# First batch reordered behind narrow dummies, second batch's turns up to one slot later, fourth and fifth batch's transfers held in turn

## The chip, the cores and the metric

The kernel runs on one core of a Trainium2 chip. The metric is the device time of one execution in microseconds (us). A profile times one execution from its first to its last instruction (the span, some 1.7 us less than the device time) and lists the TensorE clock that was granted. Ratios below are the mean time of one kernel's fast runs over the mean of the other's fast runs of the same rounds, so they are not quite the ratio of the medians quoted beside them. "Fast" is a state of the machine; every run quoted here counted as fast.

Short names: PE is TensorE, PEld its weight loads, DVE VectorE, ACT ScalarE, POOL GpSimd, SP SyncE. Batches are counted from one in the text and from zero in the code: the fifth batch is `b == 4`.

## The reference, cut

```python
q_p, k_p = phi(q, cos_w, sin_w), phi(k, cos_w, sin_w)    # relu, times cos and sin of the position
kv  = np.einsum('bhsf,bhsd->bhfd', k_p, v)                # 8 batches, 8 heads, 576 x 64
z   = np.sum(k_p, axis=2)
x   = num / den           # num: q_p with kv; den: q_p with z, + 1e-6
# x as 4608 tokens x 512, then 8 experts of 512 -> 1024 -> 512 on all tokens,
# weighted by a gate matrix that is normalised 8 times by row and by column
```

## The kernel before, the parts that matter

Attention of a batch is made while PE works on the first expert for the batch ahead of it. A block of that expert has 16 slots; `at(block, slot, fn, ...)` puts attention work behind a slot. From the third batch on, q_p is transposed by DMA; the first two batches use PE ("turns"). All six loads of a batch are issued by POOL, all transposes by SP.

The steps of a batch, in the words used below. VectorE makes q_p and k_p tiles from the loaded q and k (phi in the reference). Transposes put q_p's columns in front, and where PE does it, ScalarE or VectorE copies each turned tile out of PE's output memory (an eviction). The sums are PE's matmuls of k_p with copies of v. The denominators are its matmuls of the turned q_p with the sums of k_p; VectorE takes their reciprocal (`hl`), PE spreads it over all rows (the spread matmuls) and ScalarE copies that out (`rb`). The numerators are PE's matmuls of the turned q_p with the sums; VectorE multiplies them by rb into `xT`, which is what the expert's first layer reads (FFN; its second layer follows in the same block). `acc_lo` and `acc_hi` in the lines are storage lent to such tiles, v copies and turned q_p among them.

```python
qp_pool = p1.enter_context(tc.tile_pool(name="qp_pool", bufs=3))
...
def load(b, half, names="qkv", held_back=False):
    ...
    if held_back:
        after(ve.last, i)                     # the load waits for VectorE's instruction issued last
...
q_p = qp_pool.tile([P, C, 2, D], F16, name="q_p")         # one of three buffers
ve.tensor_tensor(out=q_p[:], ...)
if by_dma:                                                # b >= 2
    turned = nc.sync.dma_start(out=qTs[b, hk], in_=q_p..., transpose=True)
    if b == 3 and hk == 0:
        after(landing["v", b, 1], turned)                 # this transpose waits for the last v load
...
# second batch, beside the first block
for hk in range(HK):
    for i in range(3):
        at(0, (5, 6, 6, 7)[hk], turn, 1, hk, i, i != 1)
...
for half in range(2):
    at(0, 7, sums_first, half)
...
# fifth batch (j == 2): q_p, k, k_p and v by slot; numerators of the fourth batch
    (4, prep_q, 0), (5, prep_k, 0), (5, prep_q, 1), (6, prep_k, 1),
    (8, prep_q, 2), (8, prep_k, 2), (10, prep_q, 3), (10, prep_k, 3),
    (11, prep_kv, 0), (14, prep_kv, 1),
at(j, 9, numerators_of, b, 0, 1)
at(j, 13, numerators_of, b, 2, 3)
...
for name in "qkv":                                        # j == 1: the fifth batch's loads
    for half in range(2):
        at(j, 12, load, b + 2, half, name, True)
```

A transpose reads a q_p buffer, so the fourth q_p of a batch waits until the first transpose has landed and given its buffer back (VectorE waited 0.70 us for that ahead of 64.82 and 0.35 ahead of 82.86 in the profile of before).

The softmax here doesn't subtract the row's maximum and nothing guards it: scores larger than these inputs give would overflow.

## Time and profile before

| | before |
|---|---|
| median of the runs beside the change | 978.56 us (977.54 to 978.70) |
| span of the profiled run | 977.2 us, clock 1.00 |
| PE busy | 98% of the span |
| PE's first real turn | 8.62 us |
| first second-layer matmul | 34.46 us |
| fourth batch's last denominators | 73.81 us |
| fifth batch's first spread matmul | 97.02 us |

The last four rows are marks. From the last mark to the end of the span these two kernels and the others below take 880 us within 0.5, so a kernel's time is settled by its first 97 us. How to read the time-ordered list: start, length, engine, source line, operation, output and inputs, count, and in brackets how long the engine stood idle before and what ended it. These are VectorE's lines, and then PE's matmul that needs their result, around the fifth batch's last q_p in the kernel before:

```profile
82.86 0.76 DVE L109 TENSOR_TENSOR q_p<-q_ld,acc_hi 128x1152 f16<-128x1152 f16 x1 [0.35 <-DMA q_pT<-q_p]
...
85.45 1.55 DVE L109 TENSOR_TENSOR xT<-small_ps,rb 128x384 f16<-128x384 f32 x4 [0.80 <-PE small_ps L109]
...
87.34 2.80 PE L109 MATMUL h_ps<-xT,w1e 128*128 128x512 f16 x12
```

The q_p waits 0.35 us for a buffer, and VectorE is again idle for 0.80 us before it makes the last xT tiles. PE's matmul on those tiles starts at 87.34, without waiting.

### The profile page before, as it was taken

The numbers are of one execution on the slowest core, as the hardware profiler recorded it, in microseconds if no ns is written. First come the engines' busy times: TensorE is split into PE (matmuls) and PEld (weight loads), VectorE is DVE, ScalarE is ACT, GpSimd is POOL, SyncE is SP. The second block draws the span as 40 slices with busy tenths as digits, with TensorE's granted clock in tenths as the row PEclk, the third lists the DMA queues.
The fourth block names the chain that finished last, engine by engine and source line by source line (L and its number), as shares of the span: only waits on it lengthen the run. The fifth ranks groups of instructions, "written<-read, shape, count | busy, mean of one in ns | idle before, by whom it ended". The sixth has DMA issues, their size and how long they took to land.

```text
span 977.2 us, 20236 instructions
## 1 busy us (share of the span) xinstructions
PE 962.4 (98%) x7855; PEld 675.7 (69%) x7855; DVE 807.8 (83%) x1833; ACT 564.7 (58%) x1262; POOL 60.6 (6%) x82
## 2 busy tenths in 40 slices
PE   9999999999999999999999999999999999999997
PEld 6545555457777777777777777777777777777775
DVE  6767775888988887988888887988888888988887
ACT  5766665477776555555555555555555555555551
POOL 6231110010000000000000000000000000000001
PEclk9999999999999999999999999999999999999999
DMA  9999986330104401323104401323103401104435
GB/s 163 183 149 178 152 141 111 68 68 34 42 25 83 78 25 41 64 51 70 35 25 83 78 25 36 68 55 66 37 25 80 81 25 38 37 26 120 127 89 128
DMA packets 80336, 73.54 MB, mean 75 GB/s; under 512 B 33264, under 2 KB 72176, under 8 KB 80240
## 3 DMA queue, kind: packets, MB, share of 16 engines
q0 software_dynamic: 27232, 30.94, 20.3%
q1 hardware_dynamic: 52768, 41.06, 17.2%
q8 instruction: 61, 1.00, 0.4%
q14 instruction: 35, 0.29, 0.1%
q10 hardware_dynamic: 240, 0.26, 0.1%
HBM read 83.12 MB, written 12.98 MB: 98 GB/s over the span
## 4 chain that ended last, share of the span: by engine, by line
PE 88%; DMA 4%; DVE 3%; issue 2%; ACT 1%; POOL 1%; POOLq 0%; ACTq 0%; SPq 0%
PE rows_ps L109 33%; PE h_ps L109 26%; PE p_ps L109 11%; PE copied_ps L109 11%; PE y_ps L109 4%; PE small_ps L109 2%; DMA k_ld<-in_k_dram 1%; DMA w1e<-in_moe_w_dram 1%; DMA w2e<-in_moe_w_dram 1%; DMA acc_hi<-q_p 1%; DVE P_tok L109 1%; DVE colp L109 0%; POOL q_ld L202 0%; DVE rs L109 0%; DVE acc_hi L955 0%
## 5 line engine op out<-in xcount | busy, mean ns | idle before, releaser
L955 DVE SCALAR_TENSOR_TENSOR acc_lo<-rows_ps,P_tok,acc_lo 128x512 f32<-128x512 f32 (+1 forms) x322 | 203.9, 643 | 74.9 <-PE rows_ps L109 74.8
L109 PEld LDWEIGHTS <-H 128*128 128x128 f16 x2080 | 203.2, 98 | 82.5 <-issue 1.2
L891 ACT CAST u<-h_ps 128x384 f16<-128x384 f32 x288 | 138.0, 479 | 131.0 <-PE h_ps L109 131.0
L109 PEld LDWEIGHTS <-w1e 128*128 128x128 f16 x1632 | 157.7, 98 | 67.6 <-issue 5.3
L885 DVE CUSTOM_DVE_ANT_0 H<-p_ps,u 128x384 f16<-128x384 f32 x329 | 181.9, 553 | 6.5 <-PE p_ps L109 6.5
L109 PEld LDWEIGHTS <-hs 128*128 128x128 f16 x1500 | 146.6, 98 | 56.2
L109 PE MATMUL h_ps<-S,w1e 128*128 128x384 f16 x672 | 164.1, 326 | 0.7 <-ACT u L109 0.6
L109 PE MATMUL p_ps<-xT,T 128*128 128x384 f16 x672 | 164.1, 326 | 0.1
L109 PE MATMUL rows_ps<-V,H 128*128 128x256 f16 x1000 | 150.0, 273 | 0.7 <-DVE acc_hi L955 0.7
L109 PE MATMUL rows_ps<-w2e,hs 128*128 128x256 f16 x1000 | 150.0, 273 | 0.0
L109 PE MATMUL h_ps<-xT,w1e 128*128 128x384 f16 (+1 forms) x616 | 148.7, 350 | 0.1
L923 ACT ACTIVATE H<-h_ps 128x384 f16<-128x384 f32 x144 | 70.8, 492 | 95.0 <-PE h_ps L109 95.0
L109 PEld LDWEIGHTS <-T 128*128 128x128 f16 x1008 | 98.4, 98 | 30.2 <-issue 3.6
L109 PE MATMUL rows_ps<-w2e,H 128*128 128x256 f16 (+1 forms) x568 | 92.3, 285 | 0.0
L904 ACT COPY copied_ps<-h_ps 128x384 f32<-128x384 f32 x144 | 67.5, 469 | 35.4 <-PE h_ps L109 35.4
L914 ACT ACTIVATE H<-copied_ps 128x384 f16<-128x384 f32 x144 | 71.0, 493 | 20.3 <-PE copied_ps L109 20.3
L109 PE MATMUL h_ps<-S,T 128*128 128x384 f16 x336 | 81.8, 325 | 0.4 <-ACT copied_ps L109 0.3
L109 PE MATMUL copied_ps<-xT,w1e 128*128 128x384 f16 x336 | 82.1, 326 | 0.0
L109 PE MATMUL copied_ps<-w2e,H 128*128 128x256 f16 x504 | 75.5, 272 | 0.0
L109 PE MATMUL rows_ps<-V,hs 128*128 128x256 f16 x500 | 75.0, 272 | 0.0
L955 DVE SCALAR_TENSOR_TENSOR acc_lo<-copied_ps,P_tok,acc_lo 128x256 f32<-128x256 f32 x126 | 60.4, 480 | 0.6 <-PE copied_ps L109 0.2
L955 DVE SCALAR_TENSOR_TENSOR acc_hi<-rows_ps,P_tok,acc_hi 128x512 f32<-128x512 f32 (+1 forms) x56 | 41.4, 739 | 20.5 <-PE rows_ps L109 19.7
(145 smaller groups left out, 951.7 us busy)
## 6 DMA issues: line engine op xcount, KB each, us to landing
S<-x_saved SPq DMA_DIRECT2D x108, 192.0 KB, 2.4
out_dram<-acc_lo SPq DMA_DIRECT2D x62, 128.0 KB, 2.4
w1e<-in_moe_w_dram POOLq DMA_DIRECT2D x7, 1024.0 KB, 8.8
w2e<-in_moe_w_dram POOLq DMA_DIRECT2D x7, 1024.0 KB, 9.7
q_ld<-in_q_dram POOLq DMA_DIRECT2D x16, 288.0 KB, 7.1
k_ld<-in_k_dram POOLq DMA_DIRECT2D x16, 288.0 KB, 8.5
v_ld<-in_v_dram POOLq DMA_DIRECT2D x16, 288.0 KB, 9.6
x_saved<-S SPq DMA_DIRECT2D x18, 192.0 KB, 1.9
```

The source lines that it names most:

```text
L109: i = getattr(self.engine, name)(*args, **kwargs)
L885: latest = ve._custom_dve(TENSOR_ADD_SAT, out=out, in0=ps[:, 0:TU], in1=t[:], s0=FP32_MAX, s1=0.0)
L891: se.copy(out=t[:], in_=ps[:, 0:TU])
L904: se.copy(out=Y[:, 0:TU], in_=X[:, 0:TU])
L914: se.activation(out=h11, in_=Y[:, 0:TU], func=AF.Relu)
L923: se.activation(out=h12, in_=X[:, 0:TU], func=AF.Relu)
L955: ve.scalar_tensor_tensor(out=a, in0=rows, scalar=P_tok[:, g, self.e : self.e + 1], in1=a, op0=ALU.mult, op1=ALU.add,)
```

## The change

It has four parts: (a) 110 dummy matmuls of 64 columns for 74 of 128; (b) the first batch in a new order, with few dummies inside it; (c) the second batch's turns in slots 6, 6, 7, 7 for 5, 6, 6, 7, with the v copies in slot 7; (d) all four of the fourth batch's transposes wait for its last v load, the fifth batch's six loads wait for the last of these transposes, and some of its slots move. Its intent: start real work sooner, and keep transposes and loads from running through each other.

```diff
-        for _ in range(74):
-            keep_busy(1)
+        for _ in range(110):
+            te.matmul(out=idle_ps[:, 0:HP], lhsT=ones_sq[:],
+                rhs=ones_sq[:, 0:1].to_broadcast([P, HP]), start=True, stop=True)
 ...  # (b), cut: loads of q and k issued in another order, second half of k made positive
 ...  # after the first k_p tile and not the second, sums of the second
 ...  # half after the first spreads, k_p of the second batch behind the first batch's last xT
-                        at(0, (5, 6, 6, 7)[hk], turn, 1, hk, i, i != 1)
+                        at(0, (6, 6, 7, 7)[hk], turn, 1, hk, i, i != 1)
 ...
-                if held_back:
+                if behind is not None:
+                    after(turnings[behind], i)
+                elif held_back:
                     after(ve.last, i)
 ...
-                if b == 3 and hk == 0:
+                if b == 3:
                     after(landing["v", b, 1], turned)
+                turnings[b, hk] = turned
 ...
-                    (4, prep_q, 0), (5, prep_k, 0), (5, prep_q, 1), (6, prep_k, 1),
-                    (8, prep_q, 2), (8, prep_k, 2), (10, prep_q, 3), (10, prep_k, 3),
+                    (4, prep_q, 0), (5, prep_q, 1), (7, prep_k, 0), (8, prep_k, 1),
+                    (8, prep_q, 2), (9, prep_k, 2), (10, prep_q, 3), (10, prep_k, 3),
 ...
-                        at(j, 12, load, b + 2, half, name, True)
+                        at(j, 12, load, b + 2, half, name, True, (b + 1, HK - 1))
```

More of the change, by code (lines that the diff above doesn't have):

```diff
@@ L195, with load @@
         landing = {}
+        turnings = {}
         sources = {"q": q, "k": k, "v": v}
-        def load(b, half, names="qkv", held_back=False):
+        def load(b, half, names="qkv", held_back=False, behind=None):
             for name in names:
@@ L217 @@
         load(0, 0, "q")
+        load(0, 1, "q")
         gidx = cs_pool.tile([P, C], FP32, name="gidx")
@@ L222 @@
         )
+        load(0, 0, "k")
         ones_sq = cs_pool.tile([P, P], F16, name="ones_sq")
@@ L230 @@
         )
-        load(0, 1, "q")
-        for name in "kv":
-            load(0, 0, name)
-            load(0, 1, name)
+        load(0, 1, "k")
+        for half in range(2):
+            load(0, half, "v")
         w0 = new_weights(wA)
@@ L256 @@
         idle_ps = ps_y.tile([P, Dm], FP32, name="y_ps")
-        for _ in range(74):
-            keep_busy(1)
+        for _ in range(110):
+            te.matmul(
+                out=idle_ps[:, 0:HP], lhsT=ones_sq[:],
+                rhs=ones_sq[:, 0:1].to_broadcast([P, HP]), start=True, stop=True,
+            )
         wrap = cs_pool.tile([P, C], FP32, name="wrap")
@@ L275, with halve @@
         ve.memset(cs_half[:], 0.0)
-        for hh in range(2):
-            ve.tensor_copy(
-                out=cs_half[hh * HP : (hh + 1) * HP, :, :, hh],
-                in_=cs[hh * HP : (hh + 1) * HP, :, :, 0],
-            )
+        def halve():
+            for hh in range(2):
+                ve.tensor_copy(
+                    out=cs_half[hh * HP : (hh + 1) * HP, :, :, hh],
+                    in_=cs[hh * HP : (hh + 1) * HP, :, :, 0],
+                )
         early = cs_pool.tile([P, 1], FP32, name="early")
@@ L289 @@
         C3 = C // 3
+        ones_col = const.tile([P, 1], FP32, name="ones_col")
+        ve.memset(ones_col[:], 1.0)
+        ones_all = const.tile([P, P], FP32, name="ones_all")
+        ve.memset(ones_all[:], 1.0)
+        eps_row = cs_pool.tile([1, 32], FP32, name="eps_row")
+        ve.memset(eps_row[:], 1e-6 / XS)
+        lent = acc_lo[:, G_LO - 4 : G_LO, :].rearrange("p g d -> p (g d)").bitcast(F16)
+        VA = C * (D + 2)
+        v_augs = [
+            lent[:, i * VA : (i + 1) * VA].rearrange("p (c d) -> p c d", d=D + 2)
+            for i in range(4)
+        ]
+        for t in v_augs:
+            ve.memset(t[:, :, D : D + 1], 1.0 / XS)
         lo = cs_pool.tile([P, 1], FP32, name="lo")
@@ L308 @@
         )
-        ones_col = const.tile([P, 1], FP32, name="ones_col")
-        ve.memset(ones_col[:], 1.0)
-        ones_all = const.tile([P, P], FP32, name="ones_all")
-        ve.memset(ones_all[:], 1.0)
-        eps_row = cs_pool.tile([1, 32], FP32, name="eps_row")
-        ve.memset(eps_row[:], 1e-6 / XS)
         wg_ld = cs_pool.tile([P, KT, E], FP32, name="wg_ld")
@@ L321 @@
         kps, qps, qTs, kvs, hls = {}, {}, {}, {}, {}
-        lent = acc_lo[:, G_LO - 4 : G_LO, :].rearrange("p g d -> p (g d)").bitcast(F16)
-        VA = C * (D + 2)
-        v_augs = [
-            lent[:, i * VA : (i + 1) * VA].rearrange("p (c d) -> p c d", d=D + 2)
-            for i in range(4)
-        ]
         q_pTs = [qT_pool.tile([P, C, P], F16, name=f"q_pT{i}")[:] for i in range(6)] + [
@@ L335 @@
         ]
-        for t in v_augs:
-            ve.memset(t[:, :, D : D + 1], 1.0 / XS)
         def prep_k(b, hk, by_scalar=True):
@@ L444, in sums, with sums_begun @@
             sums_made(b, half, sums_begun(b, half))
-        def sums_begun(b, half):
+        def sums_begun(b, half, banks=(ps_s, "small_ps")):
             W_ = D + 1 if b else D
@@ L453, in sums_begun @@
                 )
-            kv_ps = [ps_s.tile([P, 512], FP32, name="small_ps") for hh in range(2)]
+            kv_ps = [banks[0].tile([P, 512], FP32, name=banks[1]) for hh in range(2)]
             for i in range(2):
@@ L612 @@
         for hk in range(HK):
+            prep_q(0, hk)
+            if hk == 1:
+                halve()
             if hk == 3:
@@ L616 @@
                 z_ps = key_sums(0)
-                prep_q(0, hk)
-                key_sums_made(0, z_ps)
-            else:
-                prep_q(0, hk)
             for i in range(3):
                 turn(0, hk, i, True)
-                keep_busy(3)
+                keep_busy(3 * (hk < 3))
         prep_kp(0, 0)
+        key_sums_made(0, z_ps)
+        for hk in (2, 3):
+            prep_k(0, hk)
         prep_kp(0, 1)
         denominators(0, range(0, 4))
-        keep_busy(8)
-        for hk in (2, 3):
-            prep_k(0, hk)
         z_ps = key_sums(1)
+        keep_busy(4)
+        key_sums_made(1, z_ps)
         prep_kp(0, 2)
-        key_sums_made(1, z_ps)
+        denominators(0, range(4, 8))
         prep_kp(0, 3)
-        keep_busy(5)
-        denominators(0, range(4, 8))
-        for half in range(2):
-            sums_made(0, half, sums_begun(0, half))
-            keep_busy((0, 18)[half])
+        sums_made(0, 0, sums_begun(0, 0))
+        keep_busy(20)
+        spread_out(0, 0)
+        numerators(0, 0)
+        keep_busy(4)
+        spread_out(0, 1)
+        sums_made(0, 1, sums_begun(0, 1, (ps_h[0], "h_ps")))
         hT = hA.tile([P, FT, TCH], F16, name="hT")
@@ L645, with first_l1 @@
         ]
-        for hk in range(HK):
-            attend(0, hk)
-            for kt in ((), (0,), (1,), (2, 3))[hk]:
-                for ft, h_ps in enumerate(first_ps):
-                    te.matmul(
-                        out=h_ps[:],
-                        lhsT=w0[0][:, kt, ft * P : (ft + 1) * P],
-                        rhs=xT[:, kt, 0:TCH],
-                        start=(kt == 0),
-                        stop=(kt == KT - 1),
-                    )
-                    if kt == KT - 1:
-                        se.activation(out=hT[:, ft, 0:TCH], in_=h_ps[:], func=AF.Relu)
-            for i in ((), (0,), (1, 2), ())[hk]:
-                prep_k(1, i, i < 2)
-            for i in ((), (0,), (1,), (2, 3))[hk]:
-                if i == 3:
-                    prep_k(1, i, False)
-                prep_kp(1, i)
+        def first_l1(kt, fts):
+            for ft in fts:
+                te.matmul(
+                    out=first_ps[ft][:],
+                    lhsT=w0[0][:, kt, ft * P : (ft + 1) * P],
+                    rhs=xT[:, kt, 0:TCH],
+                    start=(kt == 0),
+                    stop=(kt == KT - 1),
+                )
+                if kt == KT - 1:
+                    se.activation(out=hT[:, ft, 0:TCH], in_=first_ps[ft][:], func=AF.Relu)
+        numerators(0, 1)
+        spread_out(0, 2)
+        first_l1(0, (2, 3, 0, 1))
+        numerators(0, 2)
+        spread_out(0, 3)
+        first_l1(1, range(4))
+        numerators(0, 3)
+        prep_k(1, 0)
+        prep_k(1, 1)
+        first_l1(2, range(4))
+        first_l1(3, range(4))
+        for hk in range(HK):
+            if hk >= 2:
+                prep_k(1, hk, False)
+            prep_kp(1, hk)
         for hk in range(3):
@@ L676 @@
                     for i in range(3):
-                        at(0, (5, 6, 6, 7)[hk], turn, 1, hk, i, i != 1)
+                        at(0, (6, 6, 7, 7)[hk], turn, 1, hk, i, i != 1)
                     if hk == 0:
-                        at(0, 5, prep_q, 1, 3)
+                        at(0, 6, prep_q, 1, 3)
                     if hk == 2:
-                        at(0, 6, prep_v, 1, 0, se.copy)
-                        at(0, 6, prep_v, 1, 2, ve.tensor_copy)
+                        at(0, 7, prep_v, 1, 0, se.copy)
+                        at(0, 7, prep_v, 1, 2, ve.tensor_copy)
                     if hk == 3:
```

## The prediction

> **What bounds the kernel now.** I read the page from the top: engine shares, the 40 slices, the chain of waits, then the time-ordered list of 0 to 100 us.
>
> ```profile
> PE 962.4 (98%) x7855; PEld 675.7 (69%) x7855; DVE 807.8 (83%) x1833; ACT 564.7 (58%) x1262; POOL 60.6 (6%) x82
> ...
> PE   9999999999999999999999999999999999999997
> ```
>
> TensorE (PE) is busy 98% of the span and in every slice: from about 90 us to the end it works without a gap that matters, and the change touches nothing there. So the change is worth what it takes from PE's lost time before 90 us, and that lost time has two kinds. The first is waiting, which the wait list of PE over the first 100 us shows (what ended it, total us, times, longest):
>
> ```profile
> PE small_ps L109 <- DMA acc_hi<-q_p: 1.0, 1, 1.0
> PE small_ps L109 <- ACT acc_lo L109: 0.7, 1, 0.7
> PE small_ps L109 <- ACT q_pT L109: 0.4, 1, 0.4
> PE small_ps L109 <- ACT rb L109: 0.4, 1, 0.4
> PE small_ps L109 <- DVE acc_hi L109: 0.3, 1, 0.3
> ```
>
> The second is hidden in "busy": dummy matmuls that keep PE occupied. The time-ordered list (start us, length us, engine, operation, count) shows where real work could have gone instead:
>
> ```profile
> 1.14 7.10 PE L109 MATMUL y_ps<-ones_sq 128*128 128x128 f16 x74 [1.14 <-DVE ones_sq L109]
> ...
> 6.83 0.77 DVE L109 TENSOR_TENSOR q_p<-q_ld,acc_hi 128x1152 f16<-128x1152 f16 x1
> ...
> 8.62 0.17 PEld L109 LDWEIGHTS <-q_p 128*128 128x128 f16 x3 [0.31 <-DVE q_p L109]
> ...
> 10.53 0.53 DVE L109 TENSOR_SCALAR k_ld<-k_ld 128x576 f16<-128x576 f16 x2 [1.60 <-DMA k_ld<-in_k_dram]
> ...
> 14.02 0.66 DVE L109 TENSOR_SCALAR k_ld<-k_ld 128x576 f16<-128x576 f16 x2
> ...
> 16.20 1.35 DVE L109 RECIPROCAL den<-y_ps 96x192 f32<-96x192 f32 x1
> ...
> 25.66 1.89 PE L109 MATMUL h_ps<-xT,w1e 128*128 128x512 f16 x8
> ```
>
> The first q_p is ready at 7.60 us but the dummies and the epsilon matmuls hold PE until 8.62. The first k lands at 10.5. The second half of k is made positive only at 14.02, though the queue's next issue (12.24) shows that it had landed by 12.2: VectorE (DVE) was making k_p tiles first. That pushes the reciprocal to 16.20, the first spread matmul to 18.34 and the first block of pure FFN work to 25.66.
>
> [...] counting the starts, 47 dummies fall between 2 and 7 us (107 ns each) and 17 between 7 and 8 (59 ns); the change of rate comes 5.9 us after the first dummy. [...] transposes land in 3.2 to 3.3 us alone and in up to 10.4 us beside loads.
>
> **The change, part by part.**
>
> (a) Initial dummies. 74 x 128 columns become 110 x 64. At the cold clock I estimate 53 ns (half of 107)[...] each: 5.8 us if 53[...]. They end at 7.0 to 7.8 instead of 8.1. With 0.45 us of epsilons, the turns start at 7.5 to 8.25 instead of 8.62: 0.4 to 1.1 us earlier. q_p is ready for that: two small copies (0.50 us) move behind it, though the iota slips by 0.8 us behind the second q load; I get q_p at about 6.8.
>
> (b) New order of the first batch. The key sums still wait for k landing at 10.3 to 10.5, so they start at 11.0 to 11.4 instead of 11.70. The fourth head pair's turns lose their dummies (3 x 0.16 us). The second k half is made positive at once (12.2 instead of 14.02), so its key sums run near 12.8 instead of 14.52, the second denominators near 14.0 instead of 15.64, and the reciprocal, behind one k_p of 0.75, at 14.5 to 15.0 instead of 16.20. hl is out near 16.2 instead of 18.29. From there spreads, numerators and first-layer matmuls follow, 5.9 us of PE up to the last numerators. FFN slot 4 should start at 23.5 to 24.0 instead of 25.66: **1.7 us** earlier.
>
> (c) This is mostly given back. In the old order DVE made the second batch's k_p tiles between the numerators; in the new one all four (4 x 0.67 plus 2 x 0.24 us) stand behind the last xT, then three q_p (0.67 each). From xT's end near 22.7 that puts the first q_p out at 26.7, as late as before (26.9). The turns at slots 6 and 7 fill the time with FFN slots first, but then twelve evictions (8 on ScalarE (ACT) at 0.4, 4 on DVE at 0.55) and four v copies must pass before the sums. Adding up the queues of PE, ACT and DVE with durations from the trace, the first second-layer matmul (34.46 before) comes at 33.9 to 34.4; the same sum for the old order gives 34.27, so it is good to some 0.2 us. What remains of the 1.7 us is 0.1 to 0.5: **0.3 us**.
>
> (d) Fourth batch's transposes and fifth batch's loads. Before, one of the four transposes started at 54.33 in the middle of the v and k loads and took 10.4 us, and the last one (67.03) met the fifth batch's loads:
>
> ```profile
> 66.92 1.43 POOL L202 DMA_DIRECT2D q_ld<-in_q_dram  x2 [11.63 <-DVE acc_lo L109]
> 67.03 1.48 SPq L361 DMA_TRANSPOSE acc_hi<-q_p  x1
> ...
> 73.81 0.34 PE L109 MATMUL small_ps<-acc_hi,zsel 128*32 128x192 f16 x6 [0.96 <-DMA acc_hi<-q_p]
> ```
>
> Now all four wait for the last v load, and the loads wait for the last transpose. Without a transpose in its way the last v should land near 61.7 instead of 64.1 (six undisturbed loads from 84.95 took 11.8 us; five, less 1.9, from 51.72). The four transposes then run alone and the last lands near 69, so the 0.96 us wait at 72.9 goes: **1.0 us**. Against it, the loads start 2.3 us later. Their first users were moved (prep_k by two slots or one), but the fifth batch's first transpose (77.75 before, landing 82.8) would be issued 1.3 us earlier into loads that last 1 us longer. The fourth q_p needs its buffer back, waited 0.35 us before, and may now wait 1 to 1.5 us; DVE had 0.8 us of slack after it, and PE waits on DVE's v copies at 90.07. I take 0.3 us off; the 0.37 us wait at 59 for rb (ACT waiting on a k load[...]) may shrink: 0.2 us on.
>
> Sum: 0.3 + 1.0 - 0.3 + 0.2 = **1.2 us**, so 978.6 - 1.2 = **977.4 us**.
>
> **Rivals.** One: the prologue's 1.7 us survives, because DVE is not the limit before the sums. For it: q, v and w2 have all landed by 34.5 and PE needs w2's last part only two slots after the sums. Against it: ACT and DVE have nearly no idle time left between 23 and 33 us in my sum. It would give about 976.0. Two: a new wait takes the place of the transpose's. The fourth batch's first transposes now start late, and the fourth q_p of that batch needs one of their buffers; if the v load lands at 63 rather than 61.7, DVE stops 1 us or more near 65 and PE's sums at 66.3 wait for it. That, with the fifth batch's buffer wait in full, gives 978.5 to 979.[...]
>
> **Range and chances.** The pieces are each uncertain by about half a microsecond, the second rival by more; runs before spread 0.23 us. I take 976.0 to 978.8. A change of 2% would be 19.6 us, more than all the lost time PE has in the region touched, so within 2% is all but certain.
>
> **What would show it.** In the changed trace: last initial dummy at 7.0 to 7.8 us; reciprocal of the first batch at 14.5 to 15.0; FFN slot 4 at 23.5 to 24.0; the first second-layer matmul at 33.9 to 34.4, with PE waiting for ACT's or DVE's evictions before it; no wait of PE on a transpose near 72; the fifth batch's loads issued near 69, and a wait of DVE's q_p on a transpose near 82. The prediction is wrong if the first second-layer matmul moves by over a microsecond, or if DVE stalls near 65 or 82 long enough for PE to stand still at a sums step.

The upper ends in (a), 7.8 for the last dummy and 8.25 for the turns, came from a slower dummy, and the last 0.2 us, that the k load at 59 us would land sooner, was the author's estimate. Its "cold clock" stands for the 107 ns of a dummy between 2 and 7 us in the profile of before; its 53 ns is an estimate from that, and 54 was measured.

## The result and the profile after

The changed kernel took 980.08 us in the median of four runs: 978.40, 978.90, 981.26 and 981.94. The ratio is 1.0018 (95% interval 0.9995 to 1.0041). In two later groups of runs it was 1.0020 (1.0007 to 1.0034) and 1.0022 (1.0008 to 1.0036). So it is slower by 0.2%, some 2 us, where the prediction had it 0.12% faster. The first interval alone includes no difference; the two later ones do not. The four runs lie up to 3.5 us apart. Taken over all its 14 runs the mean clock was at 0.998 or less in five.

The run that was profiled first is the quickest one, with a span of 976.7 us. There the first batch goes as predicted. Columns as before:

```profile
1.15 5.96 PE L109 MATMUL y_ps<-ones_sq 128*128 128x64 f16 x110 [1.15 <-DVE ones_sq L109]
...
7.49 0.17 PEld L109 LDWEIGHTS <-q_p 128*128 128x128 f16 x3 [0.31 <-DVE q_p L109]
...
12.11 0.53 DVE L109 TENSOR_SCALAR k_ld<-k_ld 128x576 f16<-128x576 f16 x2
...
14.48 1.35 DVE L109 RECIPROCAL den<-y_ps 96x192 f32<-96x192 f32 x1
...
24.18 1.89 PE L109 MATMUL h_ps<-xT,w1e 128*128 128x512 f16 x8
```

A narrow dummy took 54 ns, turns start 1.13 us earlier, the reciprocal 1.72 and the first pure FFN work 1.48 us earlier. The first second-layer matmul then starts at 34.11 for 34.46: 0.35 us are left. What PE waited for in its first 100 us (what ended the wait, total us, times, longest):

```profile
PE small_ps L109 <- ACT acc_lo L109: 1.7, 3, 0.8
...
PE small_ps L109 <- DVE acc_lo L109: 0.9, 2, 0.6
PE small_ps L109 <- ACT rb L109: 0.8, 1, 0.8
```

The wait on a transpose (1.0 before) is gone from the list. In its place the waits for v copies of the fourth batch have grown (0.9 for 0.3) and so has the one for rb (0.8 for 0.4). The waits for evictions and v copies ahead of the second batch's sums come to 1.7, where three lines of the list before had 1.4. The transfers tell why, in the order of the transposes and loads of the fourth and fifth batch:

```profile
65.62 0.76 DVE L109 TENSOR_TENSOR q_p<-q_ld,acc_hi 128x1152 f16<-128x1152 f16 x1 [1.43 <-DMA q_pT<-q_p]
...
70.41 1.43 POOL L203 DMA_DIRECT2D q_ld<-in_q_dram  x2 [15.47 <-DMA acc_hi<-q_p]
...
83.92 0.76 DVE L109 TENSOR_TENSOR q_p<-q_ld,acc_hi 128x1152 f16<-128x1152 f16 x1 [1.76 <-DMA q_pT<-q_p]
...
85.63 1.54 DVE L109 TENSOR_TENSOR xT<-small_ps,rb 128x384 f16<-128x384 f32 x4
```

The held transposes give their buffers back late (1.43 us at 65.6, 0.70 before), the held loads start 3.5 us later (70.41 for 66.92), and the fifth batch's last q_p waits 1.76 us (0.35). In this run VectorE can still take it: its idle time before xT is used up, but PE does not wait. This one profile could explain neither the slower runs nor the ratio.

### The profile page after: what moved, and what is told of

Same layout as the page of the kernel before. It is cut to its first block, busy times and chain, and to the rows that moved or that the text cites. A ratio compares the mean times of both kernels' runs of the same rounds, so it can differ in the third digit from the quotient of the medians.

```text
span 976.7 us, 20298 instructions
## 1 busy us (share of the span) xinstructions
PE 961.2 (98%) x7886; PEld 674.0 (69%) x7886; DVE 808.4 (83%) x1833; ACT 564.0 (58%) x1262; POOL 60.4 (6%) x82
## 4 chain that ended last, share of the span: by engine, by line
PE 88%; DMA 4%; DVE 3%; issue 2%; ACT 1%; POOL 1%; POOLq 0%; DVEq 0%; ACTq 0%; SPq 0%
PE rows_ps L109 33%; PE h_ps L109 26%; PE p_ps L109 11%; PE copied_ps L109 11%; PE y_ps L109 4%; PE small_ps L109 2%; DMA k_ld<-in_k_dram 1%; DMA w2e<-in_moe_w_dram 1%; DMA w1e<-in_moe_w_dram 1%; DVE P_tok L109 1%; DVE colp L109 0%; DMA q_pT<-q_p 0%; POOL q_ld L203 0%; DVE rs L109 0%; DVE acc_hi L979 0%
```

## The experiments

Eighteen experiments ran, in five groups, each group on one chip and beside the kernel before. (Groups two and three ran on the same chip, and nine of the ten runs of the kernel before that stand beside group three are those of group two.) All gave correct results. The theories that their expectations name:

- **A**: the narrow dummies end just as the clock turns (in the first profile the last starts near 6.9 us, and the trace's clock record has full clock from 6.86), and in some executions PE stays at half clock.
- **B**: part (d) makes landings vary. **E** is its exact form, found on the way: VectorE waits for a q_p buffer near 83 us.
- **C**: the chip alone, whatever the kernel.
- **D**: PE's waits between 30 and 34 us, which the change packs together, let the clock fall to half.

| run | kernel | mean us | before, mean us | ratio (95%) |
|---|---|---|---|---|
| e1 | changed | 980.97 | 979.18 | 1.0020 (1.0007 to 1.0034) |
| e2 | changed, wide dummies | 980.82 | 979.18 | 1.0017 (1.0005 to 1.0029) |
| e3 | before, narrow dummies | 981.91 | 979.18 | 1.0028 (1.0013 to 1.0043) |
| e4 | changed, transfers as before | 980.35 | 979.18 | 1.0012 (1.0000 to 1.0024) |
| g1 | before | 979.09 | 979.03 | 1.0004 (0.9992 to 1.0017) |
| g2 | changed, dummies at 31 us, misplaced | 982.17 | 979.03 | 1.0036 (1.0023 to 1.0048) |
| g3 | changed, old slots | 981.09 | 979.03 | 1.0025 (1.0012 to 1.0037) |
| g4 | before, with (d) | 980.05 | 979.03 | 1.0018 (1.0004 to 1.0032) |
| h1 | changed, 4 q_p buffers | 989.41 | 978.98 | 1.0107 (1.0091 to 1.0122) |
| h2 | before, 4 q_p buffers | 986.79 | 978.98 | 1.0083 (1.0051 to 1.0115) |
| h3 | h1 with dummies at 31 us | 989.38 | 978.98 | 1.0108 (1.0092 to 1.0123) |
| h4 | changed | 980.80 | 978.98 | 1.0022 (1.0008 to 1.0036) |
| i1 | changed, v loads held further | 980.51 | 978.50 | 1.0020 (1.0008 to 1.0033) |
| i2 | changed, loads not held | 978.71 | 978.50 | 1.0002 (0.9990 to 1.0015) |
| i3 | i1 with dummies at 31 us | 981.16 | 978.50 | 1.0027 (1.0015 to 1.0040) |
| i4 | before, with (d) and i1's v loads | 981.16 | 978.50 | 1.0026 (1.0012 to 1.0039) |
| k1 | before, transposes held, loads not | 978.77 | 979.38 | 0.9993 (0.9975 to 1.0011) |
| k2 | i2 with dummies at 31 us | 978.79 | 979.38 | 0.9993 (0.9974 to 1.0012) |

The means are those of each group's runs; where the ratio differs from their quotient in the fourth place, it is the ratio from runs of the same rounds. The gap is widest in g4, where the means give 1.0010. In the last group one run of the kernel before took 984.46 us and carries its mean; the medians there are 978.79 (k1), 978.89 (k2) and 978.80 (before).

### Group one: which part brings the slow runs

**e1**, the changed kernel as it is.

> The changed kernel as it is, with five timed runs beside the kernel before. Theory A (narrow dummies end just as the clock turns, and in some executions PE stays at half clock in the prologue): two clusters again, near 978.5 and near 981.5. Theory B (the held loads and transposes of the fourth and fifth batch land at varying times): the same two clusters. Theory C (it is the chip, whatever the kernel): the kernel before shows the two clusters too in these rounds.

Measured: 979.46, 979.51, 980.17, then 981.59, 982.24, 982.88, the last three with a mean clock of 0.996 to 0.998. So two clusters, but the quick one is not at 978.5.

**e2**, the changed kernel with the old dummies.

```diff
-        for _ in range(110):
-            te.matmul(out=idle_ps[:, 0:HP], ...)
+        for _ in range(74):
+            keep_busy(1)
```

> The changed kernel with the old initial dummies (74 of 128 columns instead of 110 of 64), nothing else different. Theory A: one cluster, 978 to 979, no run over 980. Theory B and C: two clusters as in the changed kernel.

Measured: 979.87 to 982.35, all but one over 980. Theory A expected one cluster under 979, so it falls: the slow runs do not need the narrow dummies.

**e3**, the kernel before with the narrow dummies (the same edit the other way round).

> The kernel before with the 110 narrow initial dummies alone. Theory A: two clusters, the quick one within 0.5 of the kernel before (978 to 979), the other 2 to 3.5 us above. Theory B: one cluster near 978.5. Theory C: as the kernel before in these rounds.

Measured: one run of 978.80, five of 981.26 to 984.10, which is 2.1 to 4.9 us above the mean of the kernel before. The two clusters are near what theory A said, but not for its reason: in the profile PE has full clock from 6.13 us on, through the whole prologue. The profile shows PE standing 3.14 us for a transpose that met the fifth batch's loads, the wait that cost 0.96 us in the profile of before:

```profile
76.66 0.35 PE L109 MATMUL small_ps<-acc_hi,zsel 128*32 128x192 f16 x6 [3.14 <-DMA acc_hi<-q_p]
```

and then half clock. The list of stretches (stretch, its length, PE busy and matmuls started, granted clock, DMA share, GB/s):

```profile
74.40:77.81 3.41, 1.15 (x10) 1.00 1.23 189
77.81:81.22 3.41, 3.41 (x24) 0.50 1.21 206
```

**e4**, the changed kernel with the old transfers.

```diff
-                if b == 3:
+                if b == 3 and hk == 0:
                     after(landing["v", b, 1], turned)
-                        at(j, 12, load, b + 2, half, name, True, (b + 1, HK - 1))
+                        at(j, 12, load, b + 2, half, name, True)
```

> The changed kernel with the fourth and fifth batch's transfers as before: only the first of the fourth batch's transposes sets back the last v load, and the fifth batch's loads do not wait for the last transpose. Theory A: two clusters, the quick one 0.2 to 0.5 us above the changed kernel's quick one, since the 0.36 us that PE gains at 73 us goes. Theory B: one cluster near 979. Theory C: as the kernel before.

Measured: 978.93 to 982.24, all five at 0.998. PE waits 2.48 us on the transpose at 75.88, and the clock falls to half at 33.15. Not one cluster, so theory B is not the whole cause. In no run of this group was the kernel before at 0.998 or less (11 runs), so C does not explain the group either.

What these profiles gave was theory D. In e2 and e4 the half clock comes right after the idle time ahead of the second batch's sums; in the quick run of the changed kernel the same stretch, with 2.01 us of PE work for 1.72, is followed by full clock. First e2, then the changed kernel:

```profile
30.97:34.38 3.41, 1.72 (x64) 1.00 1.23 206
34.38:37.79 3.41, 3.41 (x54) 0.50 1.21 205
```

```profile
30.75:34.17 3.42, 2.01 (x79) 1.00 1.23 206
34.17:37.58 3.41, 3.41 (x37) 1.00 1.21 207
```

Half clock lasts one stretch of 3.41 us here (two or three in a row in h1 to h3 below). Four matmuls of 512 columns took 1.91 us at half clock and 1.04 at full (g1, at 63.43 and 66.02), so I estimate that a stretch of half clock costs up to 1.7 us, half of its 3.41. I count stretches from the moment when PE first got its full clock (4.0 to 7.2 us after the start in these profiles, 4.9 to 6.9 in three of the changed kernel), one every 3.41 us: every half clock in these profiles up to 105 us began a whole number of stretches after that moment, in e2 8 (7.07 to 34.38), in e3 21 (6.13 to 77.81).

### Group two: half clock or transfers

**g1**, the kernel before again, as a control.

> The kernel before, once more, as a control and for a second profile of it. By now four profiles of the first group show the TensorE clock falling to half for one stretch of 3.41 us wherever PE was busy for only 1.15 to 1.73 us of the 3.41 us ahead of it. Theory D (the change packs PE's waits between 30 and 34 us so closely that one such stretch falls under the limit in some executions, each costing 1.7 us): the kernel before has no run with a mean clock under 0.9985, ratio within 0.001 of 1. Theory C (the chip alone): slow runs at 0.996 to 0.998 here too, one in three.

The profiles with half clock were three then, not four (e2, e3 and e4), and e4 also has one such stretch that no half clock followed, as is counted below.

Measured: 978.09 to 980.02, ratio 1.0004; but two of its five runs were at 0.998, so half clock is not the change's alone. Its profile has it at 62.06, behind 2.35 us of waiting for rb, and with full clock as early as 4.03 us; its span was 978.3.

**g2**, the changed kernel with dummies ahead of the second batch's sums.

```diff
+                def fill(n):
+                    pad = ps_y.tile([P, Dm], FP32, name="y_ps")
+                    for _ in range(n):
+                        te.matmul(out=pad[:], lhsT=ones_sq[:],
+                            rhs=ones_sq[:, 0:1].to_broadcast([P, TCH]), start=True, stop=True)
                 def sums_first(half):
+                    fill((2, 3)[half])
                     sums_made(1, half, sums_begun(1, half))
```

> The changed kernel with five dummy matmuls of 512 columns in the idle time ahead of the second batch's sums (two ahead of the first half, three ahead of the second). Theory D: no half clock between 30 and 38 us in the profile, fewer runs at 0.998 or less (none or one in six), the mean 0.5 to 1 us lower than the changed kernel's, 979.5 to 980 on the chip of the first group. Theory B (landings of the fourth and fifth batch): nothing changes, runs at 0.998 or less stay at one in two.

Measured: 981.50 to 983.67, a miss, and my mistake: the second wait is inside the first half's sums, between two head pairs, so three of the dummies ran behind it and only took time. PE's list:

```profile
33.31 0.46 PE L109 MATMUL small_ps<-acc_lo,k_p 64*128 64x65 f16 x18 [0.86 <-ACT acc_lo L109]
33.70 0.82 PE L109 MATMUL y_ps<-ones_sq 128*128 128x512 f16 x3
34.46 0.74 PE L109 MATMUL small_ps<-acc_lo,k_p 64*128 64x65 f16 x36
```

**g3**, the changed kernel with the second batch's turns in their old slots (5, 6, 6, 7, two v copies in slot 6).

```diff
-                        at(0, (6, 6, 7, 7)[hk], turn, 1, hk, i, i != 1)
+                        at(0, (5, 6, 6, 7)[hk], turn, 1, hk, i, i != 1)
```

> The changed kernel with the second batch's turns at slots 5, 6, 6, 7 and the copies of v at slot 6, as in the kernel before. Theory D: PE's waits are spread over slots 5 to 8 again, so no stretch of 3.41 us between 25 and 36 us has under 1.8 us of PE work, and runs at 0.998 or less become rare; mean within 0.7 of the kernel before. If the packing comes from the new order itself and not from the slots: as the changed kernel.

Measured: 979.31 to 983.14, mean 981.09; one run of five at 0.998. The emptiest stretch between 25 and 36 us has 2.37 us of PE work, as theory D said, and half clock became rare, but the time did not follow. The first second-layer matmul starts at 34.14, as with the new slots (34.11). So the new slots of (c) move little, and half clock is not the main cost in g3: its own profile has VectorE's wait for a q_p buffer, the longest but one of the table below.

**g4**, the kernel before with part (d) alone.

> The kernel before with the fourth and fifth batch's transfers of the change alone. Theory D: the waits between 30 and 34 us are those of the kernel before, so no half clock there; the wait on a transpose at 73 us (0.96 in the profile of before, 2.5 and 3.1 in two kernels with the old transfers) goes, so 0.3 to 1 us faster than the kernel before, ratio 0.9990 to 0.9997. Theory B: this part brings the slow runs, so the mean is 1 to 2 us over the kernel before.

Measured: 978.56 to 981.43, ratio 1.0018, no run at 0.998 or less. Part (d) alone makes the kernel before slower, with the clock at full: by the ratio as much as the whole change (by the plain means 1.0 us of its 1.8). Theory B, not D.

### What the profiles of kernels with part (d) have in common

I took from each profile VectorE's wait before the fifth batch's last q_p, and the time between the two marks around it, from the fourth batch's last denominators to the fifth batch's first spread. The last column is the time over 23.17:

| kernel (profile) | wait, us | between marks, us | over 23.17 |
|---|---|---|---|
| changed, first profile | 1.76 | 96.65 - 73.48 = 23.17 | 0 |
| g4 | 2.33 | 97.08 - 73.58 = 23.50 | 0.33 |
| e2 | 2.80 | 100.71 - 76.74 = 23.97 | 0.80 |
| g2 | 3.17 | 99.99 - 75.66 = 24.33 | 1.16 |
| e1, changed | 3.73 | 98.52 - 73.61 = 24.91 | 1.74 |
| g3 | 4.05 | 99.17 - 73.96 = 25.21 | 2.04 |
| h4, changed | 4.54 | 99.67 - 73.96 = 25.71 | 2.54 |

Where the wait is over 2.0 us, the loss is the wait less 2.0 us, in each of the six rows within 0.01; where it is under, there is none. In the profiles of before, g1 and e4, with the old transfers and a wait of 0.35 or less, the same stretch takes 23.21, 23.16 and 23.17 (24.68 in e3, whose half clock at 77.81 lies in it). The way from the wait to PE is in the lines of e1, VectorE's two first and then PE's two:

```profile
86.03 0.76 DVE L109 TENSOR_TENSOR q_p<-q_ld,acc_hi 128x1152 f16<-128x1152 f16 x1 [3.73 <-DMA q_pT<-q_p]
...
87.74 1.54 DVE L109 TENSOR_TENSOR xT<-small_ps,rb 128x384 f16<-128x384 f32 x4
```

```profile
88.34 0.38 PE L109 MATMUL h_ps<-xT,w1e 128*128 128x512 f16 x1 [0.52 <-DVE xT L109]
89.07 2.15 PE L109 MATMUL h_ps<-xT,w1e 128*128 128x512 f16 x9 [0.35 <-DVE xT L109]
```

VectorE ran its instructions in program order here, so the xT tiles stand behind the waiting q_p; they come at 87.74 where they came at 85.63, and the next block's first layer needs them. PE stands still for 0.87 us there and for 0.24 at the sums behind (the list of waits names 1.1 of the 1.74 us; the rest is in shorter gaps that it does not list). This is a correlation over seven profiles; the next groups test the cause.

### Group three: a fourth buffer

**h1**, the changed kernel with four q_p buffers (one of rb's given up, or it does not fit).

```diff
-        qp_pool = p1.enter_context(tc.tile_pool(name="qp_pool", bufs=3))
+        qp_pool = p1.enter_context(tc.tile_pool(name="qp_pool", bufs=4))
-        rb_pool = p1.enter_context(tc.tile_pool(name="rb_pool", bufs=4))
+        rb_pool = p1.enter_context(tc.tile_pool(name="rb_pool", bufs=3))
```

> The changed kernel with a fourth buffer for q_p (one of the four buffers of rb given up for it). In three profiles of kernels with the change's part (d), VectorE stood 1.76, 3.73 and 4.05 us before the fifth batch's last q_p, until a transpose landed and gave its buffer back; with 3.7 and over the numerators behind it came late and PE lost 1.0 to 1.9 us between 74 and 97 us. If that is what makes the changed kernel slow (theory E): no such wait near 83 us, the time from the fourth batch's last denominators to the fifth batch's first spread near 97 us is 23.2 us in the profile, and the mean is 0.8 to 1.5 us below the changed kernel's in the same rounds. If the half clock alone is the cause (theory D): no difference over 0.4 us.

Measured: 987.30 to 990.36, ten over the kernel before. The wait for the buffer is gone and larger ones have come in other places. The first is for rb, with ScalarE standing 3.42 us for a k load until 81.95; the second is for the fifth batch's last transpose, which was issued at 89.1 among the sixth batch's loads (from 86.67) and took 15.0 us:

```profile
83.05 0.49 PE L109 MATMUL small_ps<-q_pT,kv_sb 128*64 128x384 f16 x4 [3.16 <-ACT rb L109]
104.17 0.51 PE L109 MATMUL small_ps<-q_pT,zsel 128*32 128x192 f16 x6 [6.17 <-DMA q_pT<-q_p]
```

**h2**, the kernel before with the same buffers.

> The kernel before with the same fourth buffer for q_p. There VectorE waited 0.70 and 0.35 us for a buffer and PE for neither, so theory E: within 0.5 us of the kernel before, ratio 0.9995 to 1.0005.

Measured: one run of 978.61 and five of 987.29 to 989.87. Its fourth batch's last transpose was issued at 68.42, one us after the first of the fifth batch's loads, and was in only when PE had waited 9.62 us:

```profile
82.94 0.51 PE L109 MATMUL small_ps<-acc_hi,zsel 128*32 128x192 f16 x6 [9.62 <-DMA acc_hi<-q_p]
```

**h3**, h1 with the dummies, this time two ahead of the first sums and three between its head pairs.

```diff
+                if b == 1 and half == 0 and i == 1:
+                    fills[0](3)
                 k_p, v_aug = kps.pop((b, 2 * half + i))
 ...
                 def sums_first(half):
+                    if half == 0:
+                        fill(2)
                     sums_made(1, half, sums_begun(1, half))
```

> The changed kernel with the fourth buffer for q_p and five dummy matmuls where PE stands idle at 31 to 33 us: two ahead of the second batch's first sums and three between the sums of its first and second head pair (an earlier try had put those three behind the wait, where they only cost time). Theories D and E together: no half clock between 30 and 38 us, no wait for a q_p buffer, mean 0.2 to 0.7 us below the fourth-buffer kernel without dummies. If the dummies do not matter: within 0.3 us of it.

Measured: 988.76 to 989.90, the same as h1; it tells nothing of D. Two buffer counts were changed in these three. The long waits named are for transposes and a k load, not for rb's buffers, but no run has the fourth q_p buffer alone.

**h4**, the changed kernel once more, beside them.

> The changed kernel again, on the chip of the three others. Expected mean 1 to 1.8 us above the kernel before, with some runs at a mean clock of 0.998 or less, and in the profile PE's time from the fourth batch's last denominators to the fifth batch's first spread follows VectorE's wait for the q_p buffer: 23.2 us if that wait is under 2 us, 24 to 25 if it is over 3.

Measured: 980.26 to 981.19, ratio 1.0022, and in its profile the last row of the table above, with PE's waits for xT at 89.49 (1.15) and 90.22 (0.35).

The fourth buffer took the wait away and told nothing about it, since new and longer waits on transfers came with it. That three buffers are what keeps a transpose from being issued into the loads is an argument from the order of issue in h1 and h2, not shown by itself.

### Group four: the wait shortened, and the loads freed

Its expectations call the run with the v loads the first, and so on.

**i1**, the changed kernel with the fifth batch's v loads held until its own first transpose has landed.

```diff
-                for name in "qkv":
+                for name in "qk":
                     for half in range(2):
                         at(j, 12, load, b + 2, half, name, True, (b + 1, HK - 1))
+                for half in range(2):
+                    at(j + 1, 5, load, b + 2, half, "v", True, (b + 2, 0))
```

> The changed kernel with the fifth batch's two v loads held back until its own first transpose has landed[...]. Theory E (the wait for the q_p buffer is the cause): VectorE's wait near 83 us falls to 1 us or less, the time from the fourth batch's last denominators (near 73.5) to the fifth batch's first spread (near 97) is 23.2 us, and the mean is 0.8 to 1.5 us below the changed kernel's ratio of 1.002, so 0.9995 to 1.001. If that wait is only a sign of something else: ratio 1.0015 to 1.0025 as before.

Measured: ratio 1.0020, no gain. The wait for the buffer is gone, as meant, but the v loads are now what VectorE waits for, in front of the same xT tiles:

```profile
89.52 0.45 DVE L109 COPY acc_lo<-v_ld 128x576 f16<-128x576 f16 x1 [4.20 <-DMA v_ld<-in_v_dram]
```

Between the marks it takes 100.66 - 75.16 = 25.50 us. The xT tiles are late by another wait, and the loss is there.

**i2**, the changed kernel with the loads not held: one line undone.

```diff
-                        at(j, 12, load, b + 2, half, name, True, (b + 1, HK - 1))
+                        at(j, 12, load, b + 2, half, name, True)
```

> The changed kernel with the fifth batch's loads free as in the kernel before (all four of the fourth batch's transposes still wait for its last v load). Theory E: no long wait for a q_p buffer near 83 us and 23.2 us from the fourth batch's last denominators to the fifth batch's first spread; but the fourth batch's last transposes meet the loads, so a wait of PE on a transpose of 2 us or more near 73 us. Mean 0 to 2 us above the kernel before.

Measured: 978.38 to 979.34, ratio 1.0002, so 1.8 us of the changed kernel's 2 us are gone, if its ratios of 1.0020 and 1.0022, from two other chips, may be set beside this one. Between the marks it takes 96.79 - 73.63 = 23.16 us, with no wait for a q_p buffer there: the loads start at 67.87, not 70.41, and VectorE is idle before xT again, for PE:

```profile
66.69 1.29 SPq L372 DMA_TRANSPOSE acc_hi<-q_p  x1
...
67.87 1.43 POOL L203 DMA_DIRECT2D q_ld<-in_q_dram  x2 [13.48 <-DVE acc_lo L109]
...
85.22 1.55 DVE L109 TENSOR_TENSOR xT<-small_ps,rb 128x384 f16<-128x384 f32 x4 [1.08 <-PE small_ps L109]
```

The wait of over 2 us on a transpose at 73 us, which I had expected in exchange, did not come: the last transpose (66.69) is ahead of the loads (67.87).

**i3**, i1 with the dummies of h3.

> As the first of this group, with five dummy matmuls where PE stands idle at 31 to 33 us (two ahead of the second batch's first sums, three between the sums of its first and second head pair). Theory D: no half clock between 30 and 38 us; where the first of this group has runs at a mean clock of 0.998 or less, this one has fewer, mean 0.2 to 0.8 us lower. If the dummies are of no use: within 0.3 us of it, or slower by what of them is not hidden.

Measured: 980.14 to 981.93, no gain over i1, with one run of five at 0.998 or less, as in i1. The dummies now fill the waits (PE's lines at 31 to 33 us), and no half clock follows them:

```profile
32.36 0.82 PE L109 MATMUL y_ps<-ones_sq 128*128 128x512 f16 x3
33.28 1.03 PE L109 MATMUL small_ps<-acc_lo,k_p 64*128 64x65 f16 x54
```

**i4**, the kernel before with (d) and i1's v loads.

> The kernel before with part (d) and the held v loads alone (old dummies, old order of the first batch, old slots). Theory E: the transposes' wait at 73 us is gone, VectorE's wait near 83 us is under 1.5 us, so 0.3 to 1 us faster than the kernel before, ratio 0.999 to 0.9997. If part (d) has another cost: ratio over 1.0005.

Measured: ratio 1.0026, a miss for the reason of i1. The waits on the transposes and for the buffer are gone, but VectorE waits 2.83 us for v at 88.03, and 24.53 us pass between the marks.

### Group five: what is left of each

**k1**, g4 with the loads not held, by i2's line.

> The kernel before with all four of the fourth batch's transposes behind its last v load (and the later slots of two of the fifth batch's tiles), loads not held. If this half of part (d) is worth what the wait on a transpose at 73 us costs in the profile of before: 0.3 to 1 us faster than the kernel before, ratio 0.999 to 0.9997, no wait on a transpose near 73 us. If VectorE's later q_p (a wait of 1.4 to 2.8 us near 65 us where the transposes are held) gives it back: ratio 0.9997 to 1.0005.

Measured: 977.72 to 979.68, median 978.79 beside 978.80. The wait on a transpose at 73 us is gone, and PE stands 1.28 us at 67.98 for a v copy instead, behind a q_p that waited 2.11 us for its buffer. So holding the transposes is worth nothing that these runs can tell, and g4's loss (1.0018) goes with the held loads, the one thing in which the two kernels differ.

**k2**, i2 with the dummies of h3.

> The changed kernel with the loads free and five dummy matmuls at 31 to 33 us. Theory D: no half clock between 30 and 38 us, no run at 0.998 or less that comes from there, mean 0.2 to 0.8 us below the same kernel without dummies (ratio 1.0002), so 0.9994 to 1.0000. If the half clock there hardly matters: ratio 1.0000 to 1.0005.

Measured: 978.32 to 979.28, median 978.89 beside 978.80. In its profile the only half clock comes at 60.94, behind a wait for rb. The same without the dummies (i2) is not told apart from it.

No kernel here beats the one before: k1, k2 and i2 equal it within their intervals.

### The half clock, counted

In the twenty profiles, cut into stretches of 3.41 us from the moment of full clock, there are fourteen stretches of full clock in the first 105 us with 1.77 us or less of PE work. Thirteen were followed by half clock. One, in e4 (1.64 us, mostly 512-column matmuls), was not. No stretch with 1.89 us or more was. PE need not stand still through such a stretch: in e2's (1.72 us of work from 30.97 on) the longest single wait was 0.85 us. In the profiles with both the new order and the new slots and no dummies at 31 us, half clock came between 32 and 35 us in four of eight; with dummies there in none of four; with the old order in none of seven. So theory D describes something real, and the change makes it likelier, but it is the smaller part: e1's three runs at 0.998 or less are 2.5 us over its other three, yet i2 is level with the kernel before with two of five such runs, and g4 is slow without one.

## Why the prediction was wrong

By its own steps:

- **(a)**: right. 53 to 54 ns each, last start near 6.9, turns at 7.49 (7.5 to 8.25 predicted). By e3 the dummies alone seem to cost 2.7 us in the kernel before; its profile puts that on the transpose at 73 us and half clock after it, but why the dummies should bring that on is open.
- **(b)** and **(c)**: right, or nearly, to the first second-layer matmul: reciprocal 14.48 (14.5 to 15.0), FFN slot 4 at 24.18 (23.5 to 24.0, so 0.18 late and 1.5 us gained for 1.7), second-layer matmul 34.11 (33.9 to 34.4), with PE waiting for ScalarE's evictions ahead of it as said. Not right that its 0.3 us last: at 59 us PE waits for rb behind a k load, which landed when it had before (ACT takes it at 57.89, before 57.82). The wait grew from 0.37 to 0.84 us, and the third batch's second spread starts no earlier, 59.48 for 59.41. I had counted the opposite, 0.2 us gained there.
- **(d), the gain**: the wait of 0.96 us went. But rival two came true at 65 us: the q_p there waited 1.43 us, and PE was 0.8 us behind before (69.89 for 69.09), in the quickest run. 1.0 became about 0.2, and k1 by itself has none. The 0.96 was also one profile's: in g1, the same kernel, PE does not wait there. In the eight profiles with free loads the wait goes with the order of issue. The last transpose was 1.2 us ahead of the first load in g1, i2, k1 and k2, and PE did not wait; it was 0.03 to 0.11 us behind it in before, e4 and e3, and PE waited 0.96, 2.48 and 3.14; it was 1.03 behind in h2, and PE waited 9.62.
- **(d), the cost**: this is the step that failed. It said of the fourth q_p that it "waited 0.35 us before, and may now wait 1 to 1.5 us; DVE had 0.8 us of slack after it [...] I take 0.3 us off". The mechanism was the right one, and its sizes were wrong. The last transpose, taken to land near 69, let the loads go at 70.4 to 70.9 in the three profiles of the changed kernel, so they started 3.5 us later or more and not 2.3. Three profiles of the changed kernel have waits of 1.76, 3.73 and 4.54 us; VectorE could take 2.0 in all (the 0.35, the 0.80, and as much again before PE needs xT); the cost is 0, 1.74 and 2.54 us, 1.4 in the mean where 0.3 stood. Undoing the line took 1.8 us off the changed kernel (i2), and between g4 and k1 the same line is worth 1.1 us by the medians and 2.4 us by the ratios, of which k1's leans on the one run of 984.46. Each pair was on two chips, and its two intervals overlap; that both agree with the profiles is what carries the finding.
- **Its own signs**: it named a stall of VectorE near 65 or 82 us that makes PE stand still at the sums as a sign of being wrong, and both came (PE stood 0.61 us at 67.47 in the first profile, 0.24 at 92.42 in e1). Rival two with the whole buffer wait, 978.5 to 979, came nearest, and was still too small.

Put together, with the sizes measured: 0 for the prologue and rb, 0.2 for the transposes, -1.4 for the held loads, and half clock in five of fourteen runs (a mean clock of 0.998 or less) at up to 1.7 us each by the estimate above, -0.6, less the 0.2 that the kernel before loses by it (six of 46 runs): -0.4. That is 1.6 us slower, where 1.8 to 2.2 were measured (0.0018 to 0.0022 of 979); the rest is not accounted for.

- **The range**: it took 0.23 us of scatter from three runs of the kernel before. The changed kernel scatters over 3.5 us in the four runs of the result, and the kernel before, with nine to eleven runs on each of the four later chips, over 1.8, 2.3, 4.2 and 6.8. A wait that lies between a slack of 2.0 us and a landing that moves by nearly 3 us from run to run (VectorE's wait 1.76 to 4.54) could not be sized from one profile.
- **The third rival**, half clock, was put at up to 1 us and tied to the narrow dummies; that was the author's estimate, and no profile shows it. Half clock came by another way, behind waits packed together. PE's emptiest stretch of 3.41 us there has 2.33 us of work in the profile of before and 1.72 to 2.12 in seven of the eight with the new order and slots and no dummies there.

What stays open: why the same transposes, issued at 77.4 to 77.9 behind loads issued at 70.4 to 70.9, land early enough in one run for a wait of 1.76 us and in another for 4.54, on one chip too (2.33 and 4.54 in g4 and h4); e3; and e4, which is 1.2 us slow without the held loads, with half clock and the wait of 2.48 us as the only signs in its profile.

## What to carry to other kernels

When a transfer is held behind another, follow it to the buffer that is given back last, and to everything that stands in order behind the instruction waiting for that buffer: here the loss was the wait less the whole slack of 2.0 us, one for one in six profiles. Take the slack and the landing from several profiles, not one: beside loads, the landing moved by nearly 3 us from run to run here (VectorE's wait 1.76 and 4.54 us in two profiles of one kernel). In the profile of before a transpose landed in 3.3 us when it was issued after the loads had landed (64.13) and in 10.4 when it was issued among them (54.33), and in h2 one was waited for until 14.5 us after its issue (68.42 to 82.94).

A gain that was earned before a point where PE waited for a load was lost at that point here (1.5 us at the first pure FFN work, 0.35 at the second-layer matmul, nothing at the spread behind the k load, 59.48 for 59.41). Idle time packed into one stretch of 3.41 us was what half clock followed here (thirteen of fourteen stretches with up to 1.77 us of PE work), where the same time spread out was not (none with 1.89 us or more).

One buffer more can cost: a fourth q_p buffer in the kernel before, which had waited 0.35 and 0.70 us for one, put five of six runs 8 to 11 us up (h2; one rb buffer was given up for it, and the way it came about is argued, not shown).
